# Pooled attention probabilities of batches 2 to 7: transposition by VectorE blocks and transfers in place of TensorE

## The chip, the core and the metric

The kernel runs on one core of one Trainium2 chip. The metric is device time in microseconds (us) from the first to the last instruction with what lies around it, and lower is better. TensorE (PE) multiplies matrices into PSUM banks, VectorE (DVE) and ScalarE (ACT) do element-wise work, GpSimd (POOL) helps them, and SyncE (SP) issues nearly all transfers, strictly in its program order.

## What is computed

Attention on q, k, v (8 batches, 8 heads, 576 positions, 64 wide), in two parts that are added, and behind it a two-layer network with g = h cos h.

```
q_d, k_d, v_d = mean over 4 neighbours            # 144 positions
out_d = softmax(q_d k_d^T / 8) v_d, each row repeated 4 times
out_local = softmax over |i - j| < 4 of q k^T / 8, times v
x = (out_up + out_local) as [4608, 512]
out = (h * cos(h)) @ w_out,  h = x @ w_in          # 512 -> 2048 -> 512
```

## The kernel before

The network is the bulk of the work. It takes 12 token tiles of 384 tokens; for each tile and each of 16 slices of the hidden width there is one gemm1 block (12 matmuls, L1060) and one gemm2 block (9 matmuls, L1096), in a fixed order on PE. Between them ACT, DVE and POOL turn gemm1's bank into gh and gl (L1071 to L1079).

Attention is done in units of one batch and one pair of heads, 4 per batch. Batches 0 and 1 run in the opening phase with their own code (`part_s`, `part_t`, `part_pv`, and the early branches). From batch 2 on (NEARLY = 2) a unit has three steps: `u_s` (scores and softmax), `u_t` (transposition) and `u_pv` (times v).

- `u_s`: PE computes 48 small local score matmuls (L822) and 4 pooled ones (L841), each with 72 query rows against 144 keys, into two PSUM banks. DVE takes maxima and differences (L869 to L882), ACT the exponentials (L902, L903), DVE sums, reciprocals and the multiplication by them (L907 to L923). Pooled probabilities lie in `smd`: 72 partitions, 2 heads by 2 query halves by 144 keys.
- `u_t`: DVE transposes the local ones in 32x32 blocks (L938), and SP moves them into `ptb` by four transfers (L945). The pooled ones are transposed by PE, 8 transposes of 72x72 through PSUM (L958), and brought back into `ptd` by ACT or DVE (L561, L562).
- `u_pv`: PE multiplies by the pooled values (L986) and the local ones (L1005).

A planner (`Plan.run`) sets the order of all engines by a list schedule with estimated durations; each engine then runs its list in order, so an operation whose input is late holds everything behind it on its engine. PE holds the next matmul block in the same way. SP's list holds q and k loads (L572), value loads (L593, L594), `ptb` transfers, weights read again for a check (`again`, L520) and outputs (L1118).

The kernel holds the program twice: once in the fast form (`small` true) and once in a fallback form that is entered only where a flag is set; in the trace shown here gemm1's epilogue ran 192 times, 12 tiles by 16 slices, so only the first form ran.

Of the kernel before, what the change touches and what calls it, by code (L numbers as in the profile page):

```python
# [26 lines left out]
P = 128  # L27
# [293 lines left out]
def attn_ffn_kernel(ctx: ExitStack, tc: tile.TileContext, qT, kT, vdn, vl, w_in, w_out, out, small):  # L321
# [219 lines left out]

    def ub(b, pr, name):
        shape, n, chunk, off = UNIT[name]
        if b == 1 and pr and name in "qk":
# [45 lines left out]
    def u_v(b, pr):  # L590
        pl.name = "u_v"
        vd4, vt = ub(b, pr, "vd4"), ub(b, pr, "vl")
        dma(16 * P * HD * 2, lambda: sp.dma_start(vd4.get(), vdn[b, pr].rearrange("p a r n -> p (a r) n")), w=[vd4])  # L593
# [12 lines left out]
        pl.op("POOL", 2.2, v_add(pool), w=[vd, vd4], alts=[("DVE", 1.1, v_add(dve))], shares=True)  # L606
        st[(b, pr)].update(vd=vd, vl=vt)
# [133 lines left out]
    def part_pv(b, pr, part):  # L741
# [43 lines left out]
              r=[xs], w=[done], pw=[x_b[tt]], alts=[("DVE", _dve(m / 2), lambda: dve.tensor_copy(hi(), xs.get()))])  # L785
        sub(m, lambda: x_tile(tt)[1][:, pr, a:a + m], xs.get, lambda: back(hi()), r=[xs, done], pw=[x_b[tt]])

    def u_s(b, pr, part=None):
# [4 lines left out]
        q, k, qkd = u["q"], u["k"], u["qkd"]  # L793
        sml, smd = ub(b, pr, "sml"), ub(b, pr, "smd")
# [4 lines left out]
        if b == NEARLY and pr == 0:  # L799
            zeroed.extend((pl.buf(None), pl.buf(lambda: ptb, "ptb")))  # L800

            def zero():
                pool.tensor_copy(band, mask[:, 1:2].broadcast_to([P, NSEG, BS]))
                pool.memset(band[0:BS, 0, 0:PAD], NEG)
                pool.memset(band[P - BS:P, NSEG - 1, BQ + PAD:BS], NEG)
                pool.memset(ptb, 0.0)
            pl.op("POOL", 2.5, zero, w=zeroed)
        loc, poo = [pl.buf(None) for _ in banks], [pl.buf(None) for _ in banks]

        def using(bk, o):  # L810
# [119 lines left out]
    def u_t(b, pr, part=None):  # L930
        if part is not None:
            return part_t(b, pr, part)
        pl.name = "u_t"
        u = st[(b, pr)]
        sml, smd = u["sml"], u["smd"]
        ptl, ptd = ub(b, pr, "ptl"), ub(b, pr, "ptd")

        pl.op("DVE", _dve(2 * NSEG * BS), lambda: dve.transpose(ptl.get().rearrange("p s q -> p (s q)"),  # L938
                                                                sml.get().rearrange("p s n -> p (s n)")), r=[sml], w=[ptl])
        if b >= NEARLY:  # L940
            u["ptb"] = pl.buf(lambda: ptb, "ptb")

            def move():
                for g in range(4):
                    sp.dma_start(ptb[BS * g:BS * (g + 1), g % 2], ptl.get()[BS * g:BS * (g + 1)])  # L945
            dma(8 * P * NSEG * BS, move, r=[ptl], w=[u["ptb"]])
        for h in range(2):
            bk = bank(b, "t")

            def t_mm(h=h, bk=bk):  # L950
                for kh in range(2):
                    for qh in range(2):
                        o = kh * SD + qh * HD
                        if b < NEARLY:
                            pe.matmul(bk.get()[:HD, o:o + HD], smd.get()[:, h, qh, kh * HD:(kh + 1) * HD],
                                      u["dg"].get()[:, 2 * h + qh, :], start=True, stop=True)
                            continue
                        pe.transpose(bk.get()[:HD, o:o + HD], smd.get()[:HD, h, qh, kh * HD:(kh + 1) * HD], ident[:HD, :HD])  # L958
            if b < NEARLY:
                pl.op("PE", _mm4(HD, 4), t_mm, r=[smd, u["dg"]], w=[bk], util=0.6)  # L960
            else:
                pl.op("PE", 4 * 0.061, t_mm, r=[smd], w=[bk], util=0.4)
            evac(2 * SD, lambda h=h: ptd.get()[:, h],
                 lambda bk=bk: bk.get()[:HD, :2 * SD].rearrange("p (a n) -> p a n", a=2), bk, ptd)
        u["ptl"], u["ptd"] = ptl, ptd

    def u_pv(b, pr, part=None):
# [9 lines left out]
        def d_mm():  # L977
# [70 lines left out]
    def gemm1(t, c):  # L1048
# [15 lines left out]
        tr = sb("tr", 4, [P, m], pool=fp)  # L1064
# [19 lines left out]
    def gemm2(t, c, c0, c1):  # L1084
# [19 lines left out]
        for i in range(SIZE[t] // P):  # L1104
# [2 lines left out]
                high(2)  # L1107
            pe_order(pl.op("PE", _mmr(DM, 3 - lo, small), lambda i=i: mm(i, lo, 3), r=[gh, gl, wo], w=[accs[i]]))
            if c == c1 - 1:
                bk, ob = accs[i], sb("tr", 4, [P, DM], name="ob", pool=fp)  # L1110
# [183 lines left out]
def _lay(inputs):  # L1294
    q, k, v = inputs["q"], inputs["k"], inputs["v"]

    def tr(a, front):
# [8 lines left out]
    vb = np.concatenate([  # L1306
        vb[:NEARLY].reshape(NEARLY, NPAIR, 2, NSEG // 2, 2, 4, BS, D).transpose(0, 1, 2, 4, 6, 3, 5, 7).reshape(NEARLY, NPAIR, P, -1),
        vb[NEARLY:].reshape(B - NEARLY, NPAIR, 2, NSEG, 4, BS, D).transpose(0, 1, 4, 5, 2, 3, 6).reshape(B - NEARLY, NPAIR, P, -1)])
    return {
        "qT": tr(q, 0), "kT": tr(k, PAD),  # L1310
        "vdn": np.ascontiguousarray(vp.reshape(B, NPAIR, 2, HD, 4, P).transpose(0, 1, 3, 2, 4, 5)),
        "vl": np.ascontiguousarray(vb.reshape(B, NPAIR, P, NSEG // 2, 4, D)),
        "w_in": np.ascontiguousarray(inputs["moe_w_in"]).view(np.int64),
        "w_out": np.ascontiguousarray(inputs["moe_w_out"]).view(np.int64),
# [17 lines left out]
```

## Time and profile before

| | |
|---|---|
| median of 3 executions | 958.87 us (954.58 to 961.25) |
| the profiled execution | 953.92 us |
| its span, first to last instruction | 952.1 us |
| PE busy | 926.9 us (97%) |
| DVE, ACT, POOL busy | 677.0, 641.5, 174.9 us |
| TensorE clock granted, mean of the span | 0.992 of full speed |
| share of the 16 transfer engines used by SP's queue | 30.0% |

Busy times are unions over an engine's instructions. A mean duration of a matmul contains its way through the array, so blocks are better priced from the start of one to the start of the next. The last 7.1 us hold no matmul: the outputs land there.

### The profile page before, as it was taken

The page shows a single profiled execution, that of the slowest core. Times are in us where ns is not written, and L with a number is a line of the kernel's source. Part 1 is how long each engine was busy: PE and PEld are TensorE (multiplying, and loading weights), DVE is VectorE, ACT ScalarE, POOL GpSimd, SP SyncE. Part 2 cuts the span into 40 slices and gives each one's busy share as a digit, 9 for nine tenths or more (in the row PEclk, how much of TensorE's full clock was granted, in tenths as well). Part 3 has the DMA queues.
Part 4 walks back from the last instruction along what each step waited for, and adds up shares of the span by engine and source line. Part 5 has one row for each costly group of instructions (what it writes and reads, how often), then busy time and mean ns, then how long its engine had stood idle before and what let it go on. Part 6 is the DMA issues. An engine that isn't in the chain of part 4 may idle for free.

```text
span 952.1 us, 24348 instructions
## 1 busy us (share of the span) xinstructions
PE 926.9 (97%) x10104; PEld 520.8 (55%) x10104; DVE 677.0 (71%) x1424; ACT 641.5 (67%) x1254; POOL 174.9 (18%) x243
## 2 busy tenths in 40 slices
PE   8999899999999999999999999999999999999996
PEld 5755555555556555555555555555555555555553
DVE  7799889945878768575778868665768866544443
ACT  3479778866667767675767766676767767655653
POOL 3534415411132202000003311100002220000000
PEclk9989999999999999999999999999999999999999
DMA  7881735423253422322332533413242540100001
GB/s 235 247 257 56 272 126 175 67 34 72 64 109 92 108 65 63 115 75 78 107 107 81 185 95 104 133 48 105 89 117 82 161 135 11 55 1 1 34 1 37
DMA packets 50520, 95.25 MB, mean 100 GB/s; under 512 B 5344, under 2 KB 24800, under 8 KB 50400
## 3 DMA queue, kind: packets, MB, share of 16 engines
q1 hardware_dynamic: 47808, 88.89, 30.0%
q0 software_dynamic: 2592, 4.72, 3.5%
q8 instruction: 81, 1.33, 0.6%
q14 instruction: 39, 0.32, 0.1%
HBM read 74.71 MB, written 14.16 MB: 93 GB/s over the span
## 4 chain that ended last, share of the span: by engine, by line
PE 75%; DVE 12%; DMA 5%; ACT 4%; issue 3%; SPq 1%; POOL 1%; DVEq 0%; POOLq 0%; ACTq 0%
PE bank L1060 31%; PE bank L1096 30%; PE bank L1251 2%; PE bank L822 2%; DMA k<-kT 2%; PE bank L1005 1%; PE bank L841 1%; DVE tr L1075 1%; DVE su L907 1%; DVE qkd L586 1%; PE bank L986 1%; DMA q<-qT 1%; PE bank L981 1%; DMA again<-w_in 1%; SPq L945 1%
## 5 line engine op out<-in xcount | busy, mean ns | idle before, releaser
L1096 PE MATMUL bank<-wo,gh 128*128 128x512 f16 x1152 | 343.2, 380 | 0.3 <-ACT ob L1112 0.2
L1060 PEld LDWEIGHTS <-wi 128*128 128x128 f16 x2304 | 224.3, 98 | 169.3 <-issue 6.4
L1096 PE MATMUL bank<-wo,gl 128*128 128x512 f16 x576 | 218.4, 379 | 0.0
L1075 DVE SCALAR_TENSOR_TENSOR tr<-tr,bank 128x384 f32<-128x384 f32 x192 | 104.8, 546 | 102.3 <-ACT tr L1070 101.4
L1096 PEld LDWEIGHTS <-gh 128*128 128x128 f16 x1152 | 108.3, 98 | 110.4 <-issue 4.5
L1069 ACT ACTIVATE tr<-tr 128x384 f32<-128x384 f32 x192 | 100.1, 521 | 87.6 <-DVE tr L1072 87.2
L1071 ACT ACTIVATE tr<-bank,bmagic 128x384 f32<-128x384 f32 x192 | 110.1, 574 | 62.7 <-PE bank L1060 56.5
L1072 DVE SCALAR_TENSOR_TENSOR tr<-tr,bank 128x384 f32<-128x384 f32 x192 | 105.2, 548 | 44.5 <-ACT tr L1071 43.8
L1077 ACT ACTIVATE gh<-tr 128x384 f16<-128x384 f32 x160 | 83.2, 520 | 70.9 <-DVE tr L1075 69.6
L451 DVE TENSOR_TENSOR gl<-tr,gh 128x384 f16<-128x384 f32 x147 | 84.2, 572 | 57.8 <-ACT gh L1077 55.8
L451 POOL TENSOR_TENSOR gl<-tr,gh 128x384 f16<-128x384 f32 x45 | 47.3, 1052 | 326.1 <-ACT gh L1077 177.7
L1070 ACT ACTIVATE tr<-tr 128x384 f32<-128x384 f32 x192 | 100.4, 523 | 6.1
L1060 PE MATMUL bank<-x2h,wi 128*128 128x384 f16 x384 | 101.8, 327 | 1.2 <-DVE tr L1075 1.2
L1060 PE MATMUL bank<-x3h,wi 128*128 128x384 f16 x384 | 101.5, 326 | 0.9 <-DVE tr L1075 0.9
L1060 PE MATMUL bank<-x1h,wi 128*128 128x384 f16 x384 | 101.5, 326 | 0.6 <-DVE tr L1075 0.6
L1060 PE MATMUL bank<-x0h,wi 128*128 128x384 f16 x384 | 101.5, 326 | 0.2 <-DVE tr L1075 0.2
L1096 PEld LDWEIGHTS <-gl 128*128 128x128 f16 x576 | 56.3, 98 | 68.6 <-POOL su L855 0.4
L1060 PE MATMUL bank<-x2l,wi 128*128 128x384 f16 x192 | 62.9, 327 | 0.0
L1060 PE MATMUL bank<-x0l,wi 128*128 128x384 f16 x192 | 62.7, 326 | 0.0
L1060 PE MATMUL bank<-x1l,wi 128*128 128x384 f16 x192 | 62.7, 326 | 0.0
L1060 PE MATMUL bank<-x3l,wi 128*128 128x384 f16 x192 | 62.6, 326 | 0.0
L1069 ACT ACT_TABLE_LOAD x31 | 39.8, 1283 | 0.6
(299 smaller groups left out, 1157.1 us busy)
## 6 DMA issues: line engine op xcount, KB each, us to landing
vl<-vl SPq DMA_DIRECT2D x26, 384.0 KB
out<-ob SPq DMA_DIRECT2D x36, 256.0 KB
wdi<-w_in SPq DMA_DIRECT2D x16, 512.0 KB
wdo<-w_out SPq DMA_DIRECT2D x16, 512.0 KB
again<-w_in SPq DMA_DIRECT2D x16, 512.0 KB
again<-w_out SPq DMA_DIRECT2D x16, 512.0 KB
q<-qT SPq DMA_DIRECT2D x26, 292.0 KB
k<-kT SPq DMA_DIRECT2D x26, 292.0 KB
```

Source lines behind the costliest of these rows:

```text
L451: f = lambda e: lambda: e.tensor_tensor(out=out(), in0=in0(), in1=in1(), op=ALU.subtract)
L586: pl.op("DVE", _dve(S), lambda i=i: dve.tensor_reduce(out=qkd.get()[:, i], in_=s4[i](), axis=AX.X, op=ALU.add), r=[src], pw=[qkd], alts=[( ...
L822: pe.matmul(banks[h].get()[BS * g:BS * (g + 1), c:c + BS], q.get()[hs, o:o + BS], k.get()[hs, o:o + BS], start=True, stop=True)
L1060: pe.matmul(ph.get()[:, :m], w[:, i, kc, :], x[:, kc, :], start=(n == 0), stop=(n == 3 * KC - 1))
L1069: act.activation(tr.get(), tr.get(), AF.Sin, scale=PI / fm.h)
L1070: return act.activation(tr.get(), tr.get(), AF.Square, scale=math.sqrt(fm.ratio))
L1071: pl.op("ACT", _act(m, True, 1), lambda: act.activation(tr.get(), h(), AF.Identity, bias=bmagic), r=[ph], w=[tr])
L1072: pl.op("DVE", _dve(m), lambda: dve.scalar_tensor_tensor(out=tr.get(), in0=tr.get(), scalar=MAGIC * fm.h, in1=h(), op0=ALU.subtract, op1=A ...
L1075: pl.op("DVE", _dve(m), lambda: dve.scalar_tensor_tensor(out=tr.get(), in0=tr.get(), scalar=0.5 * fm.ratio, in1=h(), op0=ALU.subtract, op1 ...
L1077: pl.op("ACT", _act(m, False), lambda: act.activation(gh.get(), tr.get(), AF.Copy), r=[tr], w=[gh], alts=[("DVE", _dve(m / 2), lambda: dve ...
L1096: pe.matmul(o, (gh, gh, gl)[k].get()[:, sl], wo.get()[:, (0, 1, 0)[k]], start=(c == c0 and k == 0), stop=(c == c1 - 1 and k == 2))
L1251: return pe.matmul(s[2].get(), ident_b, ident_b.unsqueeze(1).broadcast_to([P, 4, P]), start=True, stop=True)
```

## The change

From batch 2 on, `u_s` and `u_t` are replaced by `late_s` and `late_t`. The pooled scores of a head are now 128 query rows (four matmuls of 32 rows each, so eight for the two heads) and a last 16 query rows; the last rows of both heads share one full-width matmul against a padded operand `rest`, which POOL fills by two small copies. Probabilities lie in `prob`, 128 partitions by three planes of 160 (144 used). DVE transposes all of it in 32x32 blocks into `trn`; six transfers write `trn` to memory (`scr`) so that keys come in order, and two read it back into `ptd`, with 96 and 48 keys on the partitions. PE's transposes and the two copies out of PSUM are gone. The pooled values `vd` are laid out as 96 and 48 keys (L593's load takes 96 partitions instead of 72). The edit of the `tr` ring concerns the fallback form only.

```diff
+KH = (96, 48)
+REM = SD - P
...
+    def late_s(b, pr, u, q, k, qkd):
...
+            for g in range(4):
+                for h in range(2):
+                    hs = slice(64 * h, 64 * h + 64)
+                    pe.matmul(banks[h].get()[BS * g:BS * (g + 1), :SD], qkd.get()[hs, 0, BS * g:BS * (g + 1)], qkd.get()[hs, 1, :],
+                              start=True, stop=True)
+            pe.matmul(banks[0].get()[:, SD:2 * SD], rest, qkd.get()[:, 1, :], start=True, stop=True)
+
+        def last():
+            for h in range(2):
+                ins = pool.tensor_copy(rest[64 * h:64 * h + 64, REM * h:REM * (h + 1)], qkd.get()[64 * h:64 * h + 64, 0, P:])
+            return ins
+        rst = pl.buf(lambda: rest, "rest")
+        pl.op("POOL", 0.3, last, r=[qkd], w=[rst])
+        pl.op("PE", 1.55, mm, r=[q, k, qkd, rst], pw=banks, w=loc + poo)
...
+    def late_t(b, pr, u):
...
+        pl.op("DVE", _dve(3 * (SD + REM)), lambda: dve.transpose(trn.get().rearrange("p s q -> p (s q)"),
+                                                                smd.get().rearrange("p s n -> p (s n)")), r=[smd], w=[trn])
+        def out_():
+            for g in range(4):
+                sp.dma_start(scr.get().rearrange("h (j k) q -> k (h j) q", k=BS)[:, :, BS * g:BS * (g + 1)],
+                             trn.get()[BS * g:BS * (g + 1), :2].rearrange("p h (j q) -> p (h j) q", q=BS))
+            for h in range(2):
+                sp.dma_start(scr.get()[h, :, P:].rearrange("(j k) q -> k j q", k=BS),
+                             trn.get()[:BS, 2].rearrange("p (j q) -> p j q", q=BS)[:, :, REM * h:REM * (h + 1)])
+        def in_():
+            for i, lo in enumerate((0, KH[0])):
+                sp.dma_start(ptd.get()[:KH[i], i], scr.get()[:, lo:lo + KH[i]].rearrange("h k q -> k h q"))
+        pl.op("SP", 6 * 0.5, out_, r=[trn], w=[scr], lat=2.0)
+        pl.op("SP", 2 * 0.4, in_, r=[scr], w=[ptd], lat=2.0)
...
-                    pe.matmul(banks[0].get()[64 * h:64 * h + 64, 2 * SD:3 * SD], vd.get()[:, kh, 64 * h:64 * h + 64],
-                              ptd.get()[:, h, kh, :], start=(kh == 0), stop=(kh == 1))
+                    pe.matmul(banks[0].get()[64 * h:64 * h + 64, 2 * SD:3 * SD], vd.get()[:KH[kh], kh, 64 * h:64 * h + 64],
+                              ptd.get()[:KH[kh], kh, h, :], start=(kh == 0), stop=(kh == 1))
```

Three places show what moves. All three are of the third unit of batch 3.

The first is on PE, before: the unit's scores, then (further on) its transposes ahead of a gemm1 block, and its products with the values.

```order
L1060 MATMUL bank<-x3h,wi_1868 128x384
L822 MATMUL bank<-k,q 32x32 x48
L841 MATMUL bank<-qkd 72x144 x4
L1096 LDWEIGHTS gh
...
L1096 MATMUL bank<-wo_1875,gl 128x512
L958 MATMUL bank<-ident,smd 72x72 x8
L1060 LDWEIGHTS wi_2371
...
L986 MATMUL bank<-ptd,vd 64x144 x4
L1005 MATMUL bank<-ptb,vl 64x48 x24
```

On PE after the change the same unit reads as follows (L823, L828, L830 the scores, L1176 and L1212 gemm1 and gemm2, L1102 and L1121 the products).

```order
L1212 MATMUL bank<-wo_1374,gl 128x512
L823 MATMUL bank<-k,q 32x32 x48
L828 MATMUL bank<-qkd 32x144 x8
L830 MATMUL bank<-qkd,rest 128x144
L1176 LDWEIGHTS wi_1762
...
L1212 MATMUL bank<-wo_2230,gl 128x512
L1102 MATMUL bank<-ptd,vd 64x144 x4
L1121 MATMUL bank<-ptb,vl 64x48 x24
```

The transposes are gone, five score matmuls came in, and the products moved back: before, 36 gemm1 and 27 gemm2 matmuls stood between the unit's scores and its products, now 60 and 42.

The second place is DVE, between the pooled sums and the transposition of the local part; before:

```order
L918 RECIPROCAL su<-su 128x16
L923 TENSOR_TENSOR sml<-sml,su 128x384
L923 TENSOR_TENSOR smd<-smd,su 72x576
L938 STREAM_TRANSPOSE sml<-sml 128x384
L1075 SCALAR_TENSOR_TENSOR tr<-tr,bank 128x384
```

And the same stretch of DVE after the change, where `prob` and `trn` are the pooled probabilities before and after transposition:

```order
L871 RECIPROCAL su<-su 128x15
L874 TENSOR_TENSOR prob<-prob,su 128x3x144
L1191 SCALAR_TENSOR_TENSOR tr<-tr,bank 128x384
L883 STREAM_TRANSPOSE trn<-prob 128x480
L1194 CAST gh<-tr 128x384
L1188 SCALAR_TENSOR_TENSOR tr<-tr,bank 128x384
L455 TENSOR_TENSOR gl<-tr,gh 128x384
L899 STREAM_TRANSPOSE sml<-sml 128x384
```

A second transposition came in, and the pooled part now stands ahead of the local one.

The third place is SP's list around the unit's transfers; before, with q and k for the next unit ahead of them:

```order
L572 DMA q<-qT 128x584
L572 DMA k<-kT 128x584
L945 DMA ptb<-sml 32x384 x4
L594 DMA vl<-vl 128x768
```

And after the change (L578 loads q and k, L601 the local values):

```order
L578 DMA q<-qT 128x584
L578 DMA k<-kT 128x584
L888 DMA scr<-trn 32x10x32 x4
L891 DMA scr<-trn 32x5x16 x2
L905 DMA ptb<-sml 32x384 x4
L896 DMA ptd<-scr 96x2x144
L896 DMA ptd<-scr 48x2x144
L601 DMA vl<-vl 128x768
```

Four transfers of a unit became twelve; the two reads of `scr` wait until the six writes have landed, and everything behind them in SP's list waits with them.

## Rows read from the trace of the kernel before

**Rows 1.** Busy time by stage: length, each engine's busy us (instructions), clock, transfer share, GB/s.
```profile
0.00:135.00 135.00, 126.02 (x2366) 77.96 (x2367) 115.56 (x282) 89.61 (x213) 52.47 (x97) 0.96 0.63 199
135.00:945.00 810.00, 800.91 (x7740) 442.89 (x7737) 561.11 (x1142) 551.84 (x1041) 122.45 (x147) 1.00 0.29 84
```

**Rows 2.** Waits of PE: what waited, for whom, us in total, times, longest.
```profile
PE bank L958 <- DVE smd L923: 3.8, 5, 1.2
PE bank L1060 <- DVE tr L1075: 2.8, 8, 1.0
PE bank L1005 <- DMA ptb<-sml: 0.7, 1, 0.7
```

**Rows 3.** PE in order of time, third unit of batch 3: start us, us, instructions.
```profile
326.58 1.02 PE L822 MATMUL bank<-k,q 64*32 64x32 f32 x96
327.53 0.71 PE L841 MATMUL bank<-qkd 64*72 64x144 f32 x8
328.18 0.60 PE L1096 MATMUL bank<-wo,gh 128*128 128x512 f16 x2
...
330.13 0.33 PE L1060 MATMUL bank<-x3h,wi 128*128 128x384 f16 x1
...
332.08 0.60 PE L1096 MATMUL bank<-wo,gh 128*128 128x512 f16 x2
...
337.92 0.67 PE L958 MATMUL bank<-ident,smd 72*72 72x72 f32 x8
338.42 0.33 PE L1060 MATMUL bank<-x3h,wi 128*128 128x384 f16 x1
...
340.46 0.71 PE L986 MATMUL bank<-ptd,vd 72*64 72x144 f32 x8
341.11 0.92 PE L1005 MATMUL bank<-ptb,vl 64*64 64x48 f32 x48
341.95 0.60 PE L1096 MATMUL bank<-wo,gh 128*128 128x512 f16 x2
```

**Rows 4.** Groups by line: busy us, mean ns of one, idle before.
```profile
L879 DVE TENSOR_REDUCE mxd<-bank 72x2 f32<-72x288 f32 x56 | 24.7, 443 | 0.1
L882 DVE TENSOR_TENSOR smd<-bank,mxd 72x288 f32<-72x288 f32 x48 | 20.1, 444 | 0.0
L907 DVE TENSOR_REDUCE su<-smd 72x4 f32<-72x576 f32 x24 | 17.7, 739 | 0.1
L923 DVE TENSOR_TENSOR smd<-smd,su 72x576 f32<-72x576 f32 x24 | 17.9, 747 | 0.2
L923 DVE TENSOR_TENSOR sml<-sml,su 128x384 f32<-128x384 f32 x15 | 9.0, 602 | 0.2
L938 DVE STREAM_TRANSPOSE sml<-sml 128x384 f32<-128x384 f32 x25 | 14.3, 571 | 5.1 <-POOL sml L923 5.1
L693 DVE TENSOR_REDUCE mxd<-bank 48x1 f32<-48x144 f32 x8 | 2.3, 289 | 0.0
```

**Rows 5.** DVE in order of time, the same unit.
```profile
335.32 0.56 DVE L923 TENSOR_TENSOR sml<-sml,su 128x384 f32<-128x384 f32 x1
335.79 0.75 DVE L923 TENSOR_TENSOR smd<-smd,su 72x576 f32<-72x576 f32 x1
337.40 0.54 DVE L1072 SCALAR_TENSOR_TENSOR tr<-tr,bank 128x384 f32<-128x384 f32 x1
```

**Rows 6.** SP issuing, in order of time: start us, us, transfers.
```profile
312.76 3.78 SPq L945 DMA_DIRECT2D ptb<-sml  x4
...
319.47 0.33 SPq L594 DMA_DIRECT2D vl<-vl  x1
...
466.16 2.43 SPq L945 DMA_DIRECT2D ptb<-sml  x4
...
485.47 0.40 SPq L520 DMA_DIRECT2D again<-w_in  x1
```

**Rows 7.** PE, the one unit whose products waited for a transfer.
```profile
318.06 1.35 PE L1005 MATMUL bank<-ptb,vl 64*64 64x48 f32 x48 [0.66 <-DMA ptb<-sml]
```

**Rows 8.** Stretches by their transfers: `ptb` alone; weight reloads and some values. Columns as in 1.
```profile
466.00:471.50 5.50, 5.50 (x40) 3.06 (x38) 3.58 (x8) 3.79 (x10) 0.00 (x0) 1.00 0.14 36
780.00:786.00 6.00, 6.00 (x36) 3.31 (x34) 2.13 (x4) 2.78 (x6) 0.92 (x1) 1.00 0.71 227
```

More of the change, by code (lines that the diff above doesn't have):

```diff
@@ L330, in attn_ffn_kernel @@
     ap = ctx.enter_context(tc.tile_pool(name="ap", bufs=1))
+    dr = ctx.enter_context(tc.tile_pool(name="dr", bufs=1, space=bass.MemoryType.DRAM))
     ps = ctx.enter_context(tc.tile_pool(name="ps", bufs=1, space=bass.MemoryType.PSUM))
@@ L356, in attn_ffn_kernel @@
     ptb = const.tile([P, 2, 2 * NSEG, BS], F32, name="ptb")
+    prob, rest = const.tile([P, 3, SD + REM], F32, name="prob"), const.tile([P, P], F32, name="rest")
     def constants():
@@ L543, in ub @@
         shape, n, chunk, off = UNIT[name]
+        if b >= NEARLY and name in ("ptd", "vd4", "vd"):
+            shape = [KH[0]] + shape[1:]
         if b == 1 and pr and name in "qk":
@@ L592, in u_v @@
         vd4, vt = ub(b, pr, "vd4"), ub(b, pr, "vl")
-        dma(16 * P * HD * 2, lambda: sp.dma_start(vd4.get(), vdn[b, pr].rearrange("p a r n -> p (a r) n")), w=[vd4])
+        rows = HD if b < NEARLY else KH[0]
+        dma(16 * P * HD * 2, lambda: sp.dma_start(vd4.get(), vdn[b, pr, :rows].rearrange("p a r n -> p (a r) n")), w=[vd4])
         dma(4 * P * 12 * D, lambda: sp.dma_start(vt.get(), vl[b, pr]), w=[vt])
@@ new lines, in late_t, with move @@
+    def late_t(b, pr, u):
+        sml, smd = u["sml"], u["smd"]
+        ptl, ptd, trn = ub(b, pr, "ptl"), ub(b, pr, "ptd"), sb("smd", 1, [P, 3, SD + REM], name="trn")
+        scr = sb("scr", 2, [2, SD + REM, SD], pool=dr)
+        pl.op("DVE", _dve(3 * (SD + REM)), lambda: dve.transpose(trn.get().rearrange("p s q -> p (s q)"),
+                                                                smd.get().rearrange("p s n -> p (s n)")), r=[smd], w=[trn])
+        def out_():
+            for g in range(4):
+                sp.dma_start(scr.get().rearrange("h (j k) q -> k (h j) q", k=BS)[:, :, BS * g:BS * (g + 1)],
+                             trn.get()[BS * g:BS * (g + 1), :2].rearrange("p h (j q) -> p (h j) q", q=BS))
+            for h in range(2):
+                sp.dma_start(scr.get()[h, :, P:].rearrange("(j k) q -> k j q", k=BS),
[5 more added lines that the diff above has]
+        pl.op("SP", 2 * 0.4, in_, r=[scr], w=[ptd], lat=2.0)
+        pl.op("DVE", _dve(2 * NSEG * BS), lambda: dve.transpose(ptl.get().rearrange("p s q -> p (s q)"),
+                                                                sml.get().rearrange("p s n -> p (s n)")), r=[sml], w=[ptl])
+        u["ptb"] = pl.buf(lambda: ptb, "ptb")
+        def move():
+            for g in range(4):
+                sp.dma_start(ptb[BS * g:BS * (g + 1), g % 2], ptl.get()[BS * g:BS * (g + 1)])
+        dma(8 * P * NSEG * BS, move, r=[ptl], w=[u["ptb"]])
+        u["ptl"], u["ptd"] = ptl, ptd
@@ L793, in u_s @@
         q, k, qkd = u["q"], u["k"], u["qkd"]
+        if b >= NEARLY:
+            return late_s(b, pr, u, q, k, qkd)
         sml, smd = ub(b, pr, "sml"), ub(b, pr, "smd")
@@ L798, in u_s @@
         banks = [bank(b, "s") for _ in range(2)]
[L799 to L807, printed above, removed]
         loc, poo = [pl.buf(None) for _ in banks], [pl.buf(None) for _ in banks]
@@ L934, in u_t @@
         u = st[(b, pr)]
+        if b >= NEARLY:
+            return late_t(b, pr, u)
         sml, smd = u["sml"], u["smd"]
@@ L1062, in gemm1 @@
         pe_order(pl.op("PE", _mmr(m, 12, small), mm, r=[x_b[t], wgt[("i", c)]], w=[ph]))
-        tr = sb("tr", 4, [P, m], pool=fp)
+        tr = sb("tr", 4 if small else 2, [P, m], pool=fp)
         gh, gl = sb("gh", LAG + 1, [P, m], HP, pool=fp), sb("gl", LAG + 1, [P, m], HP, pool=fp)
@@ L1109, in gemm2 @@
             if c == c1 - 1:
-                bk, ob = accs[i], sb("tr", 4, [P, DM], name="ob", pool=fp)
+                bk, ob = accs[i], sb("tr", 4 if small else 2, [P, DM], name="ob", pool=fp)
                 pl.op("ACT", _act(DM), lambda bk=bk, ob=ob: act.activation(ob.get(), bk.get(), AF.Copy, scale=-4.0 * PI / (fm.g * fm.wo)),
@@ L1308, in _lay @@
         vb[NEARLY:].reshape(B - NEARLY, NPAIR, 2, NSEG, 4, BS, D).transpose(0, 1, 4, 5, 2, 3, 6).reshape(B - NEARLY, NPAIR, P, -1)])
+    vn, vp = np.zeros((B, NPAIR, KH[0], 2, 4, P), v.dtype), vp.reshape(B, NPAIR, SD, 4, P)
+    for x, n in ((slice(0, NEARLY), (HD, HD)), (slice(NEARLY, B), KH)):
+        vn[x, :, :n[0], 0], vn[x, :, :n[1], 1] = vp[x, :, :n[0]], vp[x, :, n[0]:]
     return {
         "qT": tr(q, 0), "kT": tr(k, PAD),
-        "vdn": np.ascontiguousarray(vp.reshape(B, NPAIR, 2, HD, 4, P).transpose(0, 1, 3, 2, 4, 5)),
+        "vdn": vn,
         "vl": np.ascontiguousarray(vb.reshape(B, NPAIR, P, NSEG // 2, 4, D)),
```

57 lines of the change are left out of this document (added).

## The prediction

> **What bounds the kernel now.** I read the busy time by stage first. After the opening 135 us PE is busy 800.9 of 810 us, while DVE stands at 561 and ACT at 552 [rows 1]. So from there on PE's own list is the time: a microsecond taken out of it is a microsecond won, and work on DVE, ACT or SP costs nothing until something makes PE wait. The waits of PE say the same: the three largest of the main stage that concern this change or the network sum to 7.3 us [rows 2]. Then I read PE in order of time around one unit, to price its blocks from start to start: scores and pooled scores 1.60 us (326.58 to 328.18), a gemm2 block 1.95, a gemm1 block 1.95, the transposes 0.50 (337.92 to 338.42), the two products 1.49 [rows 3]. There are 24 such units (six batches of four).
>
> **What leaves PE.** The transposes: 24 times 0.50 = 12.0 us. Five of these blocks also had PE waiting for the normalised probabilities, 3.8 us in all [rows 2]; those waits stand only at the transposes, so they go with them or turn up at the products, which I price below. Together 15.8 us.
>
> **What comes onto PE.** Pooled scores now take eight matmuls of 32 query rows instead of four of 72, and one full-width matmul. The trace counts every such matmul as two instructions. The old eight instructions take 0.65 us: the last starts 0.43 after the first (0.71 less about 0.28 for its own way through), 61 ns each, and 0.22 are the tail [rows 3]. The transposes, which use 72 rows and cannot stand side by side, need 63 ns for 72 columns (the last of the eight starts 0.44 after the first, 0.67 less 0.23), so one instruction of 144 columns alone costs 126 ns, and the old scores ran two at a time [rows 3]. How many run at a time with 64x32 weights is shown by the local scores: 96 instructions of 32 columns in 0.95 us, 9.9 ns each, against 28 ns for one alone, so 2.8 at a time [rows 3]. These are short, and part of their time is overhead, so 2.8 is a floor for long ones if nothing else limits them; eight distinct tiles are in the list, so eight is the ceiling. The sixteen new instructions then cost between 16 x 126 / 8 = 0.25 and 16 x 126 / 2.8 = 0.72 us, or 0.98 if only two run at a time, with the same tail of 0.22. I take 3.4 at a time, 0.60, nearer to the row than to the ceiling: 0.82 against 0.65, +0.17. The full-width matmul shares the array with nothing: two instructions of 126 ns, +0.25. Sum +0.42 per unit, 10.1 us in 24; the ends are +0.06 and +0.80 per unit, 1.4 and 19.2 us.
>
> The Trainium skill, TensorEngine Tiling (Array Packing), Key Properties, says that tiles operate independently, and lists eight tiles for 64x32. By that rule the pooled scores would take 0.25 and not 0.60 us, and the change would win 8 us more. The trace agrees only in part, since 2.8 and not eight local scores ran at a time.
>
> PE's own balance is thus -15.8 + 10.1 = -5.7 us (-14.4 to +3.4). The products keep their instruction count and columns; 96 and 48 keys in place of 72 and 72 I cost at nothing, since the columns that stream are the same.
>
> **What moves to the other engines.** DVE loses about 0.15 us in each second maximum and each second difference (443 and 444 ns become about 290, the row of 144 elements), and about 0.15 in each of sum and multiplication (739 and 747 become about 0.60, the size of the 602 ns row), 0.6 in all; it gains the second transposition, 571 ns x 480/384 = 0.71 [rows 4]. ACT loses the copies out of PSUM. POOL gets two small copies. With DVE and ACT idle 30% of the main stage [rows 1], all of this is free; what counts is when `ptd` lands.
>
> **The new chain, in one unit.** Before, in the third unit of batch 3, the reciprocal ended where the next multiplication starts, at 335.32, which is 8.7 us after the scores began [rows 3, 5]. In the new order the pooled multiplication follows at once (0.6), then one epilogue instruction (0.5), then the transposition (0.7): `trn` is ready 10.6 us after the scores began. SP then issues six writes. The nearest row is `ptb`: four transfers from 32 partitions in 2.43 us, 0.61 each [rows 6]. Six end at 14.3, the four `ptb` transfers at 16.7, the two reads at 17.4 to 17.9 (0.33 to 0.61 each). How long after its issue a transfer lands is shown once, where PE waited: issue over at 316.54, products at 318.06, so 1.5 us [rows 6, 7]. So `ptd` lands at 19.0 to 19.4. PE reaches the products 60 gemm1 and 42 gemm2 matmuls after the scores: 5 x 1.95 + 4.67 x 1.95 = 18.9, with the scores' 2.0 that is 20.9. The chain has 1.5 us to spare there, provided the writes land before SP is through with `ptb` (16.7).
>
> In 16 of the 24 units q, k or a weight reload stands in SP's list between `ptb` and the reads. A reload of 0.52 MB at 227 GB/s takes 2.3 us [rows 8], its issue 0.40 [rows 6]; the reads' bytes queue behind it and land at about 21 to 22. These units are 0 to 1 us late. I take 0.3 each, 5 us in all. The same wait takes over the place of the 3.8 us removed above.
>
> **The unknown: the price of small packets.** The writes of a unit are 1280 runs of 128 B and 320 of 64 B, 100 for each of the 16 transfer engines. No row shows such a run. In the stretch with `ptb` alone 128 packets of 1536 B took 0.14 x 16 x 5.5 = 12.3 us of engine time, 96 ns each [rows 8]. If time went with bytes, 128 B would cost 8 ns; if it didn't shrink at all, 96. The first write is in flight at 11.2; at 96 ns the last lands at 11.2 + 9.6 + 1.5 = 22.3, and `ptd` at 24.7, 3.8 us late. It breaks even near 58 ns. I take 35, because the other stretch moved packets of 1 to 4 KB at about the same cost per byte (0.71 x 16 x 6 = 68 us for 1.36 MB, 50 ns per KB, against 63 for `ptb`), so little of a packet's time looks fixed.
>
> The Trainium skill, DMA: Bandwidth & Descriptors, Specifications, says that below 512 B a transfer engine does read-modify-write. This speaks against the change; its mechanism is the first rival below, and no run here shows it yet.
>
> **Sum.** -5.7 + 5 = about -1 us against the profiled execution's 953.9, which lies 5 us under the median of the runs shown. On that median I forecast 958 us, no change: what PE saves by the transposes it spends on narrower scores and on waits for the way through memory.
>
> **Rivals.**
> - *The transfers are late* (slower). The writes of 64 and 128 B cost more than 58 ns each, and SP, in order, holds the reads and PE the products. For: the smallest packet row is 96 ns, and PE's list has at most about 2 us of slack per unit. Against: PE has six matmul blocks' worth more room between scores and products than before. At 77 ns, midway, a unit is 1.9 us late; 10 units have another's products inside their span and share that wait, so between 14 and 24 count, say 19: 36 us, 989 us in all; at 96 ns 1005 to 1045.
> - *The narrow scores overlap fully* (faster). All eight tiles at once, PE -14.4, and reads in time: 944 us. For: distinct tiles in row. Against: 2.8 in the local scores.
> - *The narrow scores overlap no better than the old ones.* PE +3.4 and 5 of waits: 967 us. For: the old scores ran exactly two at a time. Against: local scores beat it.
>
> **Chances and range.** My forecast 0.38, late transfers 0.30, full overlap 0.22, no overlap 0.10. A measurement of this kernel tells a change of about 1%, 9.6 us, from none. Full overlap is faster, 0.22; the forecast and half of the no-overlap case are within 1%, 0.42; late transfers and the rest are slower, 0.36. The forecast's own range is 950 to 966. The range for all runs from 943, just under full overlap, to 1005, the low end of 96 ns; about 0.2 is left out, mostly above.
>
> **What would show it.** The pooled scores of a unit, from their start to the next block's, should take 1.0 to 1.1 us (1.46 would be two at a time, 0.7 full overlap). PE's waits should name `ptd` with a few us in total; tens of us would be the first rival, and SP's first read would then start well over 6 us after the first write. The small packets' mean time is the transfer share of a stretch that holds one unit's writes. I would be wrong in kind if PE waited somewhere I gave no price: at POOL's copies for the padded operand, or at q and k held up behind the reads in SP's list.

## The result, and the profile of the changed kernel

The changed kernel takes 968.2 us (median of 7), the kernel before 958.6 in the same rounds. The ratio is 1.0125, 95% interval 1.0088 to 1.0162: slower by 12 us by that ratio, where I had forecast no change. The profiled execution took 964.7 us, span 962.9. Of two runs below, e5 and e9, the profiled execution was a slow one (972.3 and 962.9 us against medians of 951.6 and 943.9), with a mean clock of 0.80 and 0.84 in the opening, so from these two traces only the order and the waits behind the opening are read.

| | before | after |
|---|---|---|
| profiled execution, us | 953.9 | 964.7 |
| PE busy, of the 810 us after the opening | 800.9 | 786.6 |
| PE waits for `ptd` | none | 13.4 |
| PE waits for the second gelu step `tr` | 2.8 | 8.0 |
| VectorE waits for loads of q, k and weight reloads | 10.5 | 47.4 |

Busy time of the stage that [rows 1] show, and then two 5 us stretches of it, same columns:

```profile
135.00:945.00 810.00, 786.59 (x7730) 427.62 (x7729) 553.27 (x1131) 529.16 (x998) 121.31 (x170) 0.99 0.36 96
...
290.00:295.00 5.00, 3.36 (x62) 2.16 (x63) 4.79 (x11) 1.64 (x4) 4.35 (x7) 0.73 0.33 88
295.00:300.00 5.00, 5.00 (x16) 1.94 (x14) 3.56 (x9) 2.59 (x6) 1.22 (x2) 0.59 0.27 39
```

PE was busy for 14.3 us less of these 810 than before, so it now waits 23.4 us there instead of 9.1. The waits of PE that answer to [rows 2] (what waited, for whom, us in total, times, longest; L1176 is what L1060 was):

```profile
PE bank L1102 <- DMA ptd<-scr: 13.4, 12, 1.5
PE bank L1176 <- DVE tr L1191: 8.0, 13, 1.5
```

The 3.8 us for `smd` are gone, as the removal had it, and 13.4 for the transposed probabilities have come. I read that line first as the whole cause. The runs below show that it isn't; the decisive view is what VectorE waited for (L592 sums neighbours of q and k, L526 checks the weights that are read again), after:

```profile
DVE qkd L592 <- DMA q<-qT: 19.7, 12, 3.3
DVE odd L526 <- DMA again<-w_in: 16.7, 8, 4.0
...
DVE odd L526 <- DMA again<-w_out: 6.8, 6, 1.9
...
DVE qkd L592 <- DMA k<-kT: 4.2, 5, 1.6
```

and before:

```profile
DVE odd L522 <- DMA again<-w_in: 4.9, 2, 2.5
...
DVE qkd L586 <- DMA k<-kT: 3.0, 2, 2.4
DVE qkd L586 <- DMA q<-qT: 2.6, 3, 1.9
```

One unit shows how these hang together, the last of batch 2. SP issuing (start, us, transfers):

```profile
279.87 3.06 SPq L888 DMA_DIRECT2D scr<-trn  x4
282.98 0.95 SPq L891 DMA_DIRECT2D scr<-trn  x2
283.97 2.41 SPq L905 DMA_DIRECT2D ptb<-sml  x4
286.49 0.53 SPq L578 DMA_DIRECT2D q<-qT  x1
287.06 0.44 SPq L578 DMA_DIRECT2D k<-kT  x1
287.60 0.87 SPq L896 DMA_DIRECT2D ptd<-scr  x2
```

VectorE in the same stretch (in brackets the idle time before, and what ended it):

```profile
285.65 0.54 DVE L1188 SCALAR_TENSOR_TENSOR tr<-tr,bank 128x384 f32<-128x384 f32 x1
289.53 0.75 DVE L592 TENSOR_REDUCE qkd<-q 128x144 f32<-128x576 f32 x1 [3.34 <-DMA q<-qT]
...
292.59 0.54 DVE L1191 SCALAR_TENSOR_TENSOR tr<-tr,bank 128x384 f32<-128x384 f32 x1
```

and PE:

```profile
290.65 0.73 PE L1102 MATMUL bank<-ptd,vd 96*64 96x144 f32 x6 [1.41 <-DMA ptd<-scr]
...
293.18 0.48 PE L1176 MATMUL bank<-x2h,wi 128*128 128x384 f16 x1 [0.99 <-DVE tr L1191]
...
296.98 1.06 PE L1212 MATMUL bank<-wo,gh 128*128 128x512 f16 x2
```

SP issues in order. The load of the next unit's q stands behind all ten issues of this unit, six of them new, and starts 6.6 us after the first. VectorE, in order too, stands 3.34 us at the sum over q. The second gelu step `tr` is six instructions further in its list and ends at 293.1, and PE, which had already lost 1.41 us to `ptd`, loses 0.99 to it. So one queue delays PE on two ways: by the reads, and by the loads. After the two waits the granted clock averages 0.73 and 0.59 over the two 5 us stretches above (1 is 2.4 GHz, 0.5 is 1.2), and a pair of gemm2 matmuls takes 1.06 us instead of 0.60 [rows 3]. There are two more such places in the stage, at 515 to 525 and 760 to 765 us, each behind two waits close together; before there was none in it.

### The profile page after: what moved, and what is told of

The parts are those of the page before. It is cut to its first block, busy times and chain, and to the rows that moved or that the text cites. A ratio compares the mean times of both kernels' runs of the same rounds, so it can differ in the third digit from the quotient of the medians.

```text
span 962.9 us, 24680 instructions
## 1 busy us (share of the span) xinstructions
PE 922.0 (96%) x10150; PEld 509.8 (53%) x10150; DVE 673.0 (70%) x1423; ACT 624.0 (65%) x1222; POOL 182.4 (19%) x276
## 4 chain that ended last, share of the span: by engine, by line
PE 55%; DVE 17%; DMA 10%; ACT 6%; SPq 5%; issue 5%; POOL 2%; DVEq 0%; POOLq 0%; ACTq 0%
PE bank L1176 24%; PE bank L1212 22%; SPq L905 3%; DMA q<-qT 2%; DMA k<-kT 2%; DVE tr L1191 2%; PE bank L1367 2%; PE bank L823 1%; DMA again<-w_out 1%; DVE qkd L592 1%; DVE tr L1188 1%; DVE gl L455 1%; PE bank L1097 1%; DVE vd L610 1%; PE bank L1121 1%
## 5 line engine op out<-in xcount | busy, mean ns | idle before, releaser
L1212 PE MATMUL bank<-wo,gh 128*128 128x512 f16 x1152 | 343.5, 380 | 0.0
L1176 PEld LDWEIGHTS <-wi 128*128 128x128 f16 x2304 | 226.1, 99 | 178.7 <-issue 19.4
L1212 PE MATMUL bank<-wo,gl 128*128 128x512 f16 x576 | 218.4, 379 | 0.0
L1212 PEld LDWEIGHTS <-gh 128*128 128x128 f16 x1152 | 111.4, 98 | 112.5 <-issue 1.2
L1193 ACT ACTIVATE gh<-tr 128x384 f16<-128x384 f32 x167 | 86.9, 521 | 107.7 <-DVE tr L1191 106.8
L455 DVE TENSOR_TENSOR gl<-tr,gh 128x384 f16<-128x384 f32 x161 | 91.7, 570 | 52.3 <-ACT gh L1193 48.0
L1176 PE MATMUL bank<-x1h,wi 128*128 128x384 f16 x384 | 103.9, 333 | 2.4 <-DVE tr L1191 2.3
L1176 PE MATMUL bank<-x2h,wi 128*128 128x384 f16 x384 | 103.4, 332 | 2.7 <-DVE tr L1191 2.6
L1176 PE MATMUL bank<-x0h,wi 128*128 128x384 f16 x384 | 101.5, 326 | 2.1 <-DVE tr L1191 1.8
L1176 PE MATMUL bank<-x3h,wi 128*128 128x384 f16 x384 | 101.4, 326 | 1.6 <-DVE tr L1191 1.3
L1212 PEld LDWEIGHTS <-gl 128*128 128x128 f16 x576 | 56.5, 98 | 68.7 <-issue 0.6
L1176 PE MATMUL bank<-x1l,wi 128*128 128x384 f16 x192 | 64.1, 334 | 0.0
L1176 PE MATMUL bank<-x2l,wi 128*128 128x384 f16 x192 | 63.7, 332 | 0.0
L1176 PE MATMUL bank<-x3l,wi 128*128 128x384 f16 x192 | 62.6, 326 | 0.0
L1176 PE MATMUL bank<-x0l,wi 128*128 128x384 f16 x192 | 62.6, 326 | 0.0
L455 POOL TENSOR_TENSOR gl<-tr,gh 128x384 f16<-128x384 f32 x31 | 33.3, 1074 | 139.9 <-ACT gh L1193 121.0
L526 DVE SCALAR_TENSOR_TENSOR odd<-again,odd 128x512 int32<-128x512 int32 x32 | 22.6, 708 | 23.6 <-DMA again<-w_in 16.7
```

Source lines behind the costliest of these rows:

```text
L455: f = lambda e: lambda: e.tensor_tensor(out=out(), in0=in0(), in1=in1(), op=ALU.subtract)
L526: pl.op("DVE", 0.67, lambda: dve.scalar_tensor_tensor(out=odd.get(), in0=wd.get()[:, :, 1], scalar=0x38000000, in1=odd.get(), op0=ALU.bitw ...
L1176: pe.matmul(ph.get()[:, :m], w[:, i, kc, :], x[:, kc, :], start=(n == 0), stop=(n == 3 * KC - 1))
L1193: pl.op("ACT", _act(m, False), lambda: act.activation(gh.get(), tr.get(), AF.Copy), r=[tr], w=[gh], alts=[("DVE", _dve(m / 2), lambda: dve ...
L1212: pe.matmul(o, (gh, gh, gl)[k].get()[:, sl], wo.get()[:, (0, 1, 0)[k]], start=(c == c0 and k == 0), stop=(c == c1 - 1 and k == 2))
```

## The experiments

Ratios are to the kernel before, in the same rounds. Where a line says "order kept", every engine but those named has the very order of the kernel that the run starts from; "new plan" means that the planner laid everything anew.

| run | starts from | edit | us | ratio (95%) |
|---|---|---|---|---|
| e1 | after | reads ahead of the loads, order kept | 979.9 | 1.0288 (1.0266 to 1.0309) |
| e2 | after | products 2 us later, new plan | 956.4 | 1.0033 (0.9996 to 1.0070) |
| e3 | after | no way through memory, new plan | 941.5 | 0.9883 (0.9841 to 0.9924) |
| e4 | before | no transposes, new plan | 954.0 | 1.0001 (0.9979 to 1.0023) |
| e5 | after | loads ahead of `ptb`, order kept | 951.6 | 0.9943 (0.9909 to 0.9977) |
| e6 | after | `ptb` issued by GpSimd, order kept | 945.8 | 0.9849 (0.9800 to 0.9898) |
| e7 | before | six more writes on SP, order kept | 1000.1 | 1.0461 (1.0408 to 1.0514) |
| e8 | before | no transposes, order kept | 946.2 | 0.9881 (0.9836 to 0.9927) |
| e9 | after | planner told `ptb`'s issue time, new plan | 943.9 | 0.9867 (0.9829 to 0.9906) |
| e10 | after | as e6, and planned so, new plan | 946.7 | 0.9889 (0.9851 to 0.9927) |
| e11 | before | as e9, `ptb`'s price only, new plan | 952.8 | 0.9975 (0.9939 to 1.0010) |

The theory at the start was that the reads are late because loads stand ahead of them, and that only this makes PE wait.

**e1, reads first.**

```diff
+    for o in [o for o in order if o.name == "in_"]:     # the two reads
+        i = order.index(o)
+        while i and order[i - 1] not in [d for d, _ in o.preds] and order[i - 1].name != "move":
+            i -= 1
+        order.remove(o)
+        order.insert(i, o)                              # directly behind ptb's issues
```

> The changed kernel with one edit: on SP the two reads that bring the key-ordered probabilities back stand directly behind ptb's four issues, ahead of any load of q, k or keys that stood between. Every other engine keeps its order. Queueing theory (the reads are late because loads are issued ahead of them in SP's list and lie ahead of them in its queue): TensorE's waits for ptd fall from 13.4 us in 12 to at most 4, their landing from a median of 3.1 us to about 1.6, no stretch of the middle has a granted clock under 0.9, and the time goes from 968 to about 953 to 957 us. Rival, the trip itself (six writes, then two reads) is too long for the 20 us between scores and products: waits stay above 8 us and the time at 963 to 968. Second rival: the loads that now start later are late themselves; then waits for q, k or keys of several us appear on TensorE and the time stays above 962.

It went the other way: 979.9 us, slower than the changed kernel by 1.6%. The reads did come in time: `ptd` is no longer among the waits of PE's matmuls. But those have this line at their head,

```profile
PE bank L1176 <- DVE tr L1191: 27.6, 20, 3.1
```

and the same unit on VectorE and on PE reads

```profile
289.43 0.75 DVE L592 TENSOR_REDUCE qkd<-q 128x144 f32<-128x576 f32 x1 [3.60 <-DMA q<-qT]
...
292.47 0.54 DVE L1191 SCALAR_TENSOR_TENSOR tr<-tr,bank 128x384 f32<-128x384 f32 x1
```

```profile
289.10 0.85 PE L1121 MATMUL bank<-ptb,vl 64*64 64x48 f32 x44
293.07 0.32 PE L1176 MATMUL bank<-x2h,wi 128*128 128x384 f16 x1 [3.12 <-DVE tr L1191]
```

VectorE's waits for q, k and reloads rise from 47.4 to 57.2 us. The products start at 288.4 without a wait, and then PE stands 3.12 us for `tr`, which is late since VectorE waits for q. In the changed kernel the waits for `ptd` had hidden most of this one. With that the first theory fell: with the reads in time, the loads alone hold PE for longer than both did before. The second rival had the right place, with VectorE and not TensorE as the one that waits for the loads. The new theory: the length of SP's list is the cost, and the loads behind it count for more than the reads.

**e2, products later.**

```diff
-        pl.op("SP", 2 * 0.4, in_, r=[scr], w=[ptd], lat=2.0)
+        pl.op("SP", 2 * 0.4, in_, r=[scr], w=[ptd], lat=4.0)
```

> The changed kernel with one number changed: the planner counts the two reads as landing 4 us after their issue instead of 2, so that it puts the products some 2 us later in TensorE's list. Nothing that is issued changes otherwise. Lateness theory: waits for ptd fall from 13.4 us to under 3, no new stretch of low clock in the middle, and the time goes to about 950 to 957 us. Rival: the lateness only moves to what follows the products (x tiles, gemm1), the waits on VectorE's tr grow beyond the 8.0 us of the changed kernel, and the time stays at 961 or more.

```profile
PE bank L1176 <- DVE tr L1191: 15.5, 15, 2.3
...
PE bank L1102 <- DMA ptd<-scr: 1.5, 2, 0.9
```

Both sides had half: the waits for `ptd` went, those for `tr` doubled, and the time came to 956.4 us, level with the kernel before.

**e3, no memory trip.**

```diff
+        ptd = trn
...
-        pl.op("SP", 6 * 0.5, out_, r=[trn], w=[scr], lat=2.0)
-        pl.op("SP", 2 * 0.4, in_, r=[scr], w=[ptd], lat=2.0)
...
```

> The changed kernel without the six writes and the two reads of each unit: the products take the block-transposed tile as it lies. It leaves out bringing the keys into order, so the output is another. All transposes by VectorE, the score blocks and the copies stay. If the trip through memory is what cost the time: no wait for ptd, no low clock in the middle, and 943 to 950 us, which is below the kernel before by what the transposes took on TensorE (12 us) less the rest. Rival, VectorE's list is too crowded in the changed kernel (32x32 transposes and the x tiles): waits on tr stay at 8 us or more and the time is 955 or more.

941.5 us, a little under the 943 to 950 that I gave for the trip being the cost. No wait for `ptd`, 3.3 us for `tr`, and VectorE waits 4.8 us for q and k and none for reloads. So VectorE's list is not too crowded. What the trip costs here, 1.0125 against 0.9883, is 2.4% or 23 us, with the reserve that e3 has a new plan.

**e4 and e8, the transposes alone.** In e4 the planner lays the kernel anew without them. In e8 they issue nothing, the products take the untransposed tile, and all else stays in place:

```diff
-                for kh in range(2):
+                for kh in range(2 if b < NEARLY else 0):
...
+            if b >= NEARLY:
+                pl.op("ACT", _act(2 * SD), none, r=[bk], pw=[ptd], alts=[("DVE", _dve(2 * SD), none)])
+                continue
```

> The kernel before with, from batch 2 on, the pooled probabilities not transposed at all: the products take them as they lie. It leaves out the transposition, so the output is another; scores stay in their old form. This prices the removal by itself: 24 x 0.50 us on TensorE and 3.8 us of waits, so 958.6 to about 943 us (940 to 946). Rival, the removed work was cover for other waits or its end on TensorE: under 8 us gained, 951 or more.

> The kernel before with the pooled transposes and their copies left out from batch 2 on, and every other instruction in exactly the order of the kernel before (the run before this one let the planner make a new plan). It leaves out the transposition, so the output is another. If the removal is worth what the timeline says (24 x 0.50 us and 3.8 us of waits): 938 to 944 us against 954.7. Rival, the time goes into other waits of the same order: 950 to 955.

e4 gained nothing, e8 1.2%: 11.4 us (7.0 to 15.7) of the 15.8 that the removal was to bring. In e8 the waits for `smd` are gone, and more than them stands elsewhere:

```profile
PE bank L1067 <- DVE tr L1082: 9.6, 12, 3.0
```

against 2.8 before [rows 2]. That e4 differs from e8 by 1.2% shows what a new plan can do by itself. Its profiled opening had a mean clock of 0.91 (before 0.96), but runs that keep the changed kernel's order differ there as well (0.97 in e1, 0.80 in e5, 0.96 in the changed kernel), so why that plan is worse stays open. e3, with the new scores, the transpositions by VectorE and the copies, has the same ratio as e8 (0.9883 and 0.9881): no cost of these other parts shows, but e3 has a new plan and e8 the old order, so this isn't as firm as the figures look.

**e5, loads ahead of ptb.** The test of the new theory with the smallest edit. The reads stay where they are; only the loads that stood between them and `ptb`'s issues change places with those issues.

```diff
+    for m in [o for o in order if o.name == "move"]:    # ptb's four issues
+        ...
+        for o in [o for o in order[i:j] if o.eng == "SP" and o is not m]:
+            ...
+                order.insert(max(i, at_), o)            # ahead of them
```

> The changed kernel with one edit: in the 16 units where loads of q, k or keys stand on SP between ptb's four issues and the two reads, they stand ahead of ptb's issues, directly behind the six writes. Every other engine keeps its order; the reads stay where they were. Theory SP-list (SP issues in order, so the loads reach the queue late, VectorE waits for them, and what stands behind on VectorE, the second gelu step tr, holds TensorE): VectorE's waits for q, k and again fall from 47 us to 15 to 25, TensorE's waits on tr from 8 to 4 or less, those on ptd stay near 13, and the time goes from 968 to 960 to 964 us. Rival, only the products' wait counts (VectorE has slack for its loads): 966 to 970.

951.6 us, 17 us faster than the changed kernel by ratio, and faster than the kernel before (0.9909 to 0.9977): well past what I expected. SP in the same unit, which comes 24 us later in this execution:

```profile
303.99 3.09 SPq L888 DMA_DIRECT2D scr<-trn  x4
307.12 0.94 SPq L891 DMA_DIRECT2D scr<-trn  x2
308.10 0.43 SPq L578 DMA_DIRECT2D q<-qT  x1
308.58 0.43 SPq L578 DMA_DIRECT2D k<-kT  x1
309.11 2.42 SPq L905 DMA_DIRECT2D ptb<-sml  x4
311.63 0.53 SPq L896 DMA_DIRECT2D ptd<-scr  x1
```

and the waits:

```profile
DVE qkd L592 <- DMA q<-qT: 9.5, 10, 1.7
...
PE bank L1176 <- DVE tr L1191: 5.6, 8, 1.8
...
PE bank L1102 <- DMA ptd<-scr: 3.1, 4, 1.7
```

VectorE's waits for q, k and reloads fall from 47.4 to 21.4 us. What I had not expected is that the reads profit as well: issued just as far back, they land in a median of 2.2 us instead of 3.0, probably because the loads' bytes now move while SP issues `ptb`, and are out of the way when the reads come (in e1, with no load ahead of the reads, the median is 2.1). So PE's waits for `ptd` fell too, from 13.4 to 3.1 us, where I had expected them to stay, and e5 by itself does not part the loads from the reads. That VectorE has no slack for its loads is what e1 shows.

**e6, ptb issued by GpSimd.**

```diff
-                sp.dma_start(ptb[BS * g:BS * (g + 1), g % 2], ptl.get()[BS * g:BS * (g + 1)])
+                pool.dma_start(ptb[BS * g:BS * (g + 1), g % 2], ptl.get()[BS * g:BS * (g + 1)])
```

> The changed kernel with ptb's four transfers of each unit issued by GpSimd at the same place of the program instead of SP, whose list gets some 2.4 us shorter in each of 24 units; the rest of the order is kept. Theory SP-list: loads and reads both come 2.4 us earlier, TensorE's waits on ptd fall from 13.4 to under 4, VectorE's waits for loads from 47 us to about 20, no low clock in the middle, 950 to 957 us. Rival: GpSimd issues them so slowly or so late that the products wait for ptb instead (over 8 us), or GpSimd's own work (gl, x tiles, sums of q and k) gets late; then 963 or more.

```profile
PE bank L1176 <- DVE tr L1191: 4.2, 9, 0.8
...
PE bank L1102 <- DMA ptd<-scr: 1.0, 2, 0.8
```

and from the view of the tile `ptb` its issues (count, shortest, median and longest in ns, first and last start):

```profile
L905 POOL DMA_DIRECT2D ptb<-sml x96: 498/505/747, 151.6 to 799.5; - x96
```

945.8 us, 2.7% under the changed kernel by ratio, under the kernel before as well, and better than the 950 to 957 that I expected. PE waits 1.0 us for `ptd`, there is no stretch of low clock in the main stage (135 to 945 us), and VectorE waits 16.3 us for q, k and reloads. The same bytes move, so it is not their amount that costs. SP's list is shorter, but `ptb` also goes by another queue now (it lands in a median of 3.3 us instead of 1.9), and this run alone does not part the two; e9 below keeps all on SP. GpSimd needs a median of 505 ns for an issue, SP 588.

The Trainium skill, DMA: Bandwidth & Descriptors, Issuing engines are not separate DMA queues, says that issuing from several engines saves only the issuing time, "which is usually small relative to the DMA itself". Nothing in this run speaks against the first half; the second does not fit this kernel, where four issues take 2.4 us of SP and each transfer lands in a median of 1.9.

**e7, six writes added to the kernel before.** Parts of the transposed tile `ptl`, in the sizes of the new writes, to memory, read by nobody.

```diff
...
+                for g in range(4):
+                    sp.dma_start(scr[BS * g:BS * (g + 1), :, :BS], ptl.get()[BS * g:BS * (g + 1), :10])
+                for h in range(2):
+                    sp.dma_start(scr[:BS, 5 * h:5 * h + 5, BS:BS + 16], ptl.get()[:BS, :5, :16])
```

> The kernel before with six more transfers behind ptb's four in each unit of batch 2 on: parts of the same transposed tile, in the changed kernel's sizes, written to memory and read by nobody. Every other engine keeps its order. It prices six issues on SP by themselves (some 2.8 us each time). Theory SP-list: VectorE's waits for q, k and again grow from 10 us to 25 or more, TensorE's waits on tr grow by several us, and the time goes from 954.7 to 959 to 966 us. Rival, the loads have enough lead: 953 to 956.

1000.1 us: the direction of the theory, and several times its size. No work of PE, VectorE or ACT was added. The six issues take more of SP here than in the changed kernel (by the medians of one issue 3.6 us a unit against 2.7). VectorE waits 44.3 us for q, k and reloads, 10.5 before. One unit on VectorE, on PE, and the line of PE's waits:

```profile
294.88 0.75 DVE L587 TENSOR_REDUCE qkd<-q 128x144 f32<-128x576 f32 x1 [3.59 <-DMA q<-qT]
...
298.99 0.75 DVE L924 TENSOR_TENSOR smd<-smd,su 72x576 f32<-72x576 f32 x1
```

```profile
299.88 1.14 PE L964 MATMUL bank<-ident,smd 72*72 72x72 f32 x8 [3.08 <-DVE smd L924]
```

```profile
PE bank L964 <- DVE smd L924: 17.3, 8, 3.6
```

The same chain: q behind the issues, VectorE held, and behind it the multiplication on which the transposes wait. I had left out that in this kernel PE has two places that wait for VectorE, with 17.3 us here and 9.5 at `tr`, against 3.8 and 2.8 before [rows 2]. I had left out the clock too: nine 5 us stretches behind the opening have a mean under 0.9, none in the same stage of the kernel before. The one behind the wait of 3.08 us:

```profile
300.00:305.00 5.00, 5.00 (x21) 2.59 (x20) 2.84 (x6) 2.16 (x5) 2.25 (x4) 0.50 0.11 29
```

**e9, e10 and e11, the planner's price.** The planner counts a transfer as bytes over 262 GB/s, which makes `ptb`'s four issues 0.75 us; SP needs 2.4. In 16 of the 24 units of the changed kernel it laid loads between these issues and the reads; with the prices of e9 it does so in none.

```diff
-        pl.op("SP", 2 * 0.4, in_, r=[scr], w=[ptd], lat=2.0)
+        pl.op("SP", 2 * 0.4, in_, r=[scr], w=[ptd], lat=3.1)
...
-        dma(8 * P * NSEG * BS, move, r=[ptl], w=[u["ptb"]])
+        dma(2.4 * 262e3, move, r=[ptl], w=[u["ptb"]])
```

> The changed kernel, all transfers on SP, with two numbers of the planner put to what the trace shows: ptb's four issues count 2.4 us of SP instead of 0.75, and the two reads land 3.1 us after their issue instead of 2. The plan is made anew from that. Theory SP-list, and that the planner laid the loads behind ptb because it held those issues for short: VectorE's waits for q, k and again fall from 47 us to under 25, TensorE's waits for ptd to under 4, and the time is 947 to 957 us. Rival, the planner has no better place for the loads (q and k come free only once the scores are done): 960 or more.

> As the run with ptb on GpSimd, but the planner knows it: ptb's four issues stand on GpSimd with 2.1 us (505 ns each were measured) and land 2.8 us later, the two reads land after 3.1 us. A candidate for a kernel that beats both. Theory SP-list: no wait of TensorE for ptd or ptb over 2 us in all, VectorE's waits for loads at most those of the run it builds on (16 us), 938 to 948 us. Rival, a new plan gives away in the opening what it gains in the middle (the low clock of the opening differs from plan to plan): 948 to 958.

> The kernel before with only the planner's price of ptb's four issues put from 0.75 to 2.4 us of SP; nothing is computed otherwise. It asks what of the gain of the priced changed kernel (943.9 us) belongs to the price alone. If in the kernel before VectorE waits little for q, k and again (10 us in all), there is little to gain: 950 to 957 us, and the change with the price is then worth about 1.2 per cent. Rival, the price would have made the kernel before as fast: 940 to 948.

e9 takes 943.9 us with all transfers on SP, better than the 947 to 957 that I expected. Its waits:

```profile
DVE qkd L592 <- DMA q<-qT: 11.5, 10, 2.8
...
PE bank L1102 <- DMA ptd<-scr: 1.6, 1, 1.6
```

The rival is refuted: a better place for the loads exists. Which of the two prices did more was not tried. e5 and e9 issue on SP all that the changed kernel does, so what costs is not the length of SP's list by itself but which loads stand behind the issues. The same price of `ptb` in the kernel before (the second of the two edits; there are no reads there) changes nothing that can be measured (e11), so with the price right on both sides the change is worth 0.9867/0.9975, 1.1% or some 10 us. e10 brings nothing beyond e6. e6, e9 and e10 lie within each other's intervals, and all three beat both kernels.

## Why the prediction was wrong

**The transposes.** Of the 15.8 us for the removal e8 shows 11.4 (7.0 to 15.7). The text said the waits of 3.8 us would go or turn up at the products; 6.8 us more turned up at `tr`. With the 12.0 for the blocks that leaves 9.0, inside the interval.

**The scores.** Mis-sized: +10.1 us in the sum, about nothing measured. PE in the unit of [rows 3], after:

```profile
325.76 0.99 PE L823 MATMUL bank<-k,q 64*32 64x32 f32 x94
326.56 0.32 PE L828 MATMUL bank<-qkd 64*32 64x144 f32 x2
326.58 0.21 PE L823 MATMUL bank<-k,q 64*32 64x32 f32 x2
326.59 0.51 PE L828 MATMUL bank<-qkd 64*32 64x144 f32 x14
327.03 0.51 PE L830 MATMUL bank<-qkd,rest 128*128 128x144 f32 x2
327.38 0.33 PE L1176 MATMUL bank<-x3h,wi 128*128 128x384 f16 x1
```

From the scores' start to the next block 1.62 us, as in most of the units, 1.60 before. From the first pooled score it is 0.82 us (326.56 to 327.38), where the text gave 1.0 to 1.1 for the forecast and 0.7 for full overlap. The sixteen narrow instructions hold the array for 0.47 us (326.56 to 327.03), 29 ns each, so 4.3 at a time by the 126 ns that I had for one. I had taken 3.4. The larger part is at the joints: the first narrow one starts 0.80 us after the local scores instead of 0.95, before the last of the local scores has started, and the full-width matmul's 0.35 includes the tail of 0.22 that I had charged to the narrow ones as well.

**Small packets.** The first rival is refuted. In the stretch with this unit's writes and most of its `ptb`,

```profile
336.00:340.50 4.50, 4.50 (x27) 2.41 (x26) 3.73 (x8) 3.74 (x8) 0.00 (x0) 1.00 0.34 54
```

the engines were busy for 0.34 x 16 x 4.5 = 24.5 us, `ptb`'s share included; over 1600 small packets that is at most some 15 ns each; I took 35, and the break-even was 58. SP waited for the writes to land 0.9 us in the whole run.

**The chain of a unit** held in seven of the eight units where no load stands in it; in the eighth PE waited 0.65 us. In the unit of [rows 3] the reads' issue was over at 342.45, 16.7 us after the scores began, against 17.4 to 17.9 in the text, and PE didn't wait. (With the text's own terms `ptd` would land at 18.9 at the earliest, not 19.0; nothing hangs on it.)

**The failed step** is the one headed by the 16 units with a load between `ptb` and the reads. It asked what the loads do to the reads, and priced that at 5 us, 0 to 1 us late in a unit; the trace has 12.8 us in ten of these units, up to 2.2 in one. It did not ask what the six new issues do to the loads behind them. That way is enough by itself: e1 and e2 take the reads' lateness away, and PE's waits for `tr` go from 8.0 to 27.6 and 15.5 us. e5 moves the loads forward by some 2.4 us and wins 17, with both kinds of wait shorter. The step rests on a sentence further up, that work on DVE, ACT or SP costs nothing until PE waits. True, but SP's list was not idle where it mattered; six issues more in each unit cost the kernel before 44 us (e7). The last paragraph had named q and k held up behind the reads in SP's list as a place without a price, with PE as the one that would wait. They stand behind the writes and `ptb` as well; VectorE is what waits for them, and it reaches PE as `tr`. Nor had I priced what waits do to the clock.

So the sum: the removal brings about 11 us, scores, transpositions and copies nothing that showed, and the trip costs about 23 (from e3, so with its new plan in it). That is the price of the trip in the order that the planner had given it, not of the trip as such: e9, with the trip, has 0.9867, as low as e3 without it (0.9883). How these 23 divide into the waits for `ptd`, those for `tr` and the stretches of low clock was not taken apart, since they follow from one another. The clock is observed behind the waits, and no run here changed it alone.

## What to carry to other kernels

Where a step is moved to transfers, price the issuing queue by its issues as the trace shows them, and list what stands behind them in that queue: each load there can be late by up to their sum, and the engine that waits for it may be another than the one that the change speaks of. A wait that tops the list can be the cover of another one with the same cause, so move the cause and not the waiter. Where a planner sets the order, put its price for the moved work to the measured one before the change is judged.

## What the runs showed of the hardware that I had not expected

- Four issues of 48 KB each from 32 partitions take SP 2.4 us. A read of 108 KB lands in a median of 3.0 us in the changed kernel, where loads are issued just ahead of it in 16 of 24 units, in 2.1 in e1, where none are, and in 2.2 in e5, where `ptb`'s issues lie between.
- Writes of 64 and 128 B runs cost a transfer engine at most some 15 ns each.
- The first narrow matmuls with 64x32 weights (326.56) started before the last local scores of the block ahead (326.58); by their spacing of 29 ns against 126 for one alone, about four ran at a time.
- The granted clock does not follow from a wait's length alone. After 1.41 and 0.99 us in the changed kernel it stood at 0.73 and 0.59. In e1 it stayed at 1.00 behind the single wait of 3.12 us that ended at 293.07, and went to 0.66 behind one of 2.06 that ended at 310.26:

```profile
295.00:300.00 5.00, 5.00 (x134) 2.88 (x132) 4.81 (x13) 3.23 (x7) 1.93 (x3) 1.00 0.31 51
...
310.00:315.00 5.00, 4.74 (x18) 2.13 (x18) 4.54 (x11) 3.84 (x8) 2.61 (x4) 0.66 0.95 128
```
